# A chunked delta-rule attention with two MLPs on one Trainium2 core: the first group of chunks in another order, and nine idle-time matmuls during its inverse

## The chip, the cores and the metric

One core of a Trainium2 chip runs the whole program. The metric is device time in microseconds (us) of one execution, as a median of several; the profile is of one execution of its own.

## The reference, cut to what matters

```python
# attention: batch 4, heads 8, sequence 768, head size 48
for t in range(S):
    kt, vt, bt = (k_n[:, :, t], v[:, :, t], beta[:, :, t, None])
    y[:, :, t] = np.einsum('bhd,bhde->bhe', q[:, :, t], state)
    v_old = np.einsum('bhde,bhd->bhe', state, kt)
    state = state + bt[:, :, :, None] * np.einsum('bhd,bhe->bhde', kt, vt - v_old)
...
# first MLP: 8 experts over all 3072 tokens, weighted by a Sinkhorn-normalised gate P
for e in range(E):
    h = np.maximum(x @ w1[e], 0.0)
    ye = h @ w2[e]
    out += P[:, e:e + 1] * ye
...
# second MLP
h = x @ w_in
g = h * (1.0 / (1.0 + np.exp(-1.702 * h)))
return (g @ w_out).astype(np.float32)
```

k_n is k divided by its norm. The attention is a recurrence over the tokens; both MLPs take all 3072 tokens.

## The kernel before

The attention goes in 24 chunks `u` of 64 tokens, and the chunks in six groups `g` of four. All heads of two batches are taken together, on the upper and the lower 64 partitions. Two pieces of program make it up.

- `prep(g)` makes, for the four chunks of a group, the inverse of a triangular matrix. `gram` multiplies keys with keys and with queries on TensorE (tile `pg`); the scores times the mask `bm` go to `am` (`take`, L188), and the products with the queries to the planes of `x` (L199), which GpSimd masks later (`mask_m`, L207). The lower blocks of `am` are copied beside the diagonal (L266), a VectorE transpose makes `ln` (L269), and 30 steps of two VectorE instructions each, `lt` (L279) and `ln` (L283), invert the blocks. Two more transposes make `ta` (L314) and `tt` (L340); small matmuls `pz` (L323) and `px` (L332), each followed by ScalarE copies, finish the inverse in `tt`.
- `chain(u)` is the recurrence itself, in four stages: `ks` (keys times state, L373) and the right side `r` on VectorE (L375; in a first chunk minus `v`, on ScalarE, L379); `up` (inverse times `r`, L384) and its copies to `su`; `sp` (keys times `su`, L395) and the new state `S` (L399, L401); `y` (L408) and its copy `ys`. Each stage needs the one before it.

When chunk u is in work, the output of chunk u-1 is transposed (`xt`, L421) and split into two float32r parts `xb` (L495 on ScalarE, L496 on VectorE). From it come the gate's logits (`pl`) and the first expert (`expert0`, tiles `ph`, `po`), cut into items of three matmuls. Before expert 0 its weights are split: ScalarE casts them, and VectorE subtracts (L545, tiles `w1s`, `w2s`) in four sets of four instructions; `split0` is a call for the next set.

The order of the instructions on each engine is the order in which Python issues them. `slot(t)` runs once per stage of a chunk (t = 4u + stage), takes a number of pieces from `prep` and puts expert items between them. For t up to 15 that number is `FIRST[t]`, afterwards `PIECES[t % 16]`. `self.at` ties some calls to a step of the inverse, by group and step: (0, 20) issues the score products of chunks 4 to 7 ahead, into PSUM tiles that expert 0 uses later (`early`), and `kept[v]` is the masking that takes them.

Group 0 runs ahead of the loop, up to the first `px`; the rest of its pieces, in the list below, and group 1 come between the stages of the first four chunks:

```python
((pz, 0, 8), (tr, None), (tr, 0, 0, 8), (tr, 64, 0, 8), (px, 0, 8), (tr, 0, 8, 24),
 (tr, 64, 8, 24), (pz, 8, 8), (px, 8, 8), (pz, 16, 16), (px, 16, 16))
```

Here `pz` and `px` name a first block and a number of blocks; eight blocks are one chunk. The attention is followed by seven experts and the second MLP, which fill the rest of the time with large matmuls.

Of the kernel before, what the change touches and what calls it, by code (L numbers as in the profile page):

```python
# [9 lines left out]
F32 = mybir.dt.float32  # L10
# [11 lines left out]
H = 8  # L22
D = 48
# [5 lines left out]
PIECES = (4, 2, 2, 1, 2, 4, 4, 4, 4, 4, 4, 4, 3, 3, 2, 2)  # L29
ITEMS = (6, 5, 5, 5, 5, 5, 5, 5, 5, 5, 5, 6, 5, 5, 5, 5)  # L30

FIRST = (0, 4, 3, 2, 2, 2, 2, 3, 3, 4, 5, 5, 5, 4, 4, 4)


LAG = 10
# [5 lines left out]
class Attention:  # L41
# [130 lines left out]
    def gram(self, u, planes, h0, n, pool=None):  # L172
# [21 lines left out]
        if planes[-1] == 1:  # L194
            for b in range(2):
# [4 lines left out]
                else:  # L200
                    nc.vector.tensor_tensor(out=m, in0=ps[p, :, len(planes) - 1], in1=bm[p, hs], op=ALU.mult)

    def mask_m(self, u):
        for b in range(2):
            p = slice(64 * (1 - b), 64 * (1 - b) + 64)
            m = self.X[u // 2 % 4][p, 1 + b, u % 2]
            self.nc.gpsimd.tensor_tensor(out=m, in0=m, in1=self.bm[u][p], op=ALU.mult)  # L207

    def prep(self, g):

        nc, am, tt = self.nc, self.am, self.tt
        w, u = 2 * g, 4 * g
        if g == 0:
            self.square(0, nc.vector)
            self.square(1, nc.vector)
            self.norm(0)
            self.norm(1)
            self.weigh(0, 1)
            self.mask(0, eng=nc.vector)
            for v in range(1, 4):  # L220
                self.mask(v)
            for v in range(4):
                self.gram(v, (0,), 0, H, (self.psc, "c") if v < 2 else None)
            self.scale_v(0)
            self.scale_k(0)
            self.square(2)
            self.square(3)
            self.at = {(0, 13): lambda: [self.gram(v, (1,), 0, H) for v in range(4, 8)],
                       (0, 20): lambda: self.kept.update({v: self.gram(v, (0,), 0, H, self.early[v - 4])
                                                          for v in range(4, 8)}),  # L230
                       (0, 23): lambda: self.split0(), (1, 4): lambda: self.split0(), (1, 10): lambda: self.split0()}
            yield 1.0
        elif g == 1:
            self.weigh(2, 3)
            nc.gpsimd.tensor_copy(out=self.gate, in_=self.w[3][:, 1, 7:8])
            self.scale_k(1)
            self.mask_m(2)
            self.mask_m(3)
            yield 1.0
            for v in range(4, 8):  # L240
                self.mask(v, eng=nc.vector)
                self.kept[v]()
                if v % 2:
                    self.split0()
                yield 1.0
        else:
            for i in range(8):
                if i == 5:
                    self.mask(u + 3)
                self.gram(u + i // 2, (0, 1), i % 2 * 4, 4)  # L250
                if i == 1:
                    self.square(w + 1)
                elif i == 2:
                    self.norm(w + 1)
                elif i == 3:
                    self.weigh(w + 1)
                    self.mask(u + 2)
                elif i == 7:
                    self.scale_k(w)
                    self.scale_k(w + 1)  # L260
                yield 1.0
# [1 line left out]
        ln = self.one.tile([128, 32, 32], F32, tag="ln", name="ln")  # L263

        for q in (32, 96):
            (nc.vector.tensor_copy if g == 0 and q == 32 else nc.scalar.copy)(  # L266
                out=am[q:q + 32, :, 0:32], in_=am[q:q + 32, :, 32:64])
            yield 1.0
        nc.vector.transpose(out=ln, in_=am[:, :, 0:32].rearrange("p m t -> p t m"))  # L269
        if g == 0:  # L270
# [4 lines left out]
        for jj in range(1, 31):  # L275
# [4 lines left out]
                out=t3, in0=ln[:, jj + 1:32, jj:jj + 1].to_broadcast([128, nr, jj]),  # L280
# [47 lines left out]
        def px(m0, n):  # L328
# [6 lines left out]
            for q in (0, 64):  # L335
                nc.scalar.copy(out=tt[q:q + 32, m0:m0 + n, 32:64], in_=ps[q:q + 32])

        def tr(q, m0=0, n=32):
            if q is None:
                nc.vector.transpose(out=tt[:, :, 32:64].rearrange("p m t -> p t m"), in_=ln)  # L340
            else:
                nc.scalar.copy(out=tt[q:q + 32, m0:m0 + n, 0:32], in_=tt[q:q + 32, m0:m0 + n, 32:64])

        for f, *i in (((pz, 0, 16), (tr, None), (pz, 16, 16), (tr, 0), (tr, 64), (px, 0, 16), (px, 16, 16)) if g else
                      ((pz, 0, 8), (tr, None), (tr, 0, 0, 8), (tr, 64, 0, 8), (px, 0, 8), (tr, 0, 8, 24),
                       (tr, 64, 8, 24), (pz, 8, 8), (px, 8, 8), (pz, 16, 16), (px, 16, 16))):
            while f == tr and self.upped < u - 1:
                yield 1.0
            f(*i)
            if f == px and i[0] == 0:  # L350
                self.ready = g
                if g == 0:
                    self.norm(2)
                    self.norm(3)
            yield 1.0

    def chain(self, u):

        nc = self.nc
# [3 lines left out]
        x, tt, bk = self.X[w % 4], self.tt, self.bk[w % 4]  # L363
        tk = [slice(64, 128), slice(0, 64)]
        S = self.S
        r = self.wk.tile([128, H, D], F32, tag="r", name="r", bufs=1)

        su = self.wk.tile([128, 2, H, D], F32, tag="su", name="su", bufs=1)
        if not first:
            ks = self.psc.tile([128, H, D], F32, tag="c", name="ks")  # L370
            for h in range(H):
                for b in range(2):
                    nc.tensor.matmul(ks[tk[b], h], x[64 * b:64 * b + D, 0, j, h], S[64 * b:64 * b + D, h],  # L373
                                     start=True, stop=True)
            nc.vector.tensor_tensor(out=r, in0=ks, in1=self.V[w][:, j], op=ALU.subtract)  # L375
            nc.scalar.copy(out=su[0:64, 0], in_=S[0:64])
            nc.scalar.copy(out=su[64:64 + D, 1], in_=S[64:64 + D])
        else:
            nc.scalar.mul(r, self.V[w][:, j], -1.0)  # L379
        yield  # L380
        up = self.psc.tile([128, H, D], F32, tag="c", name="up")
# [7 lines left out]
        if not last:  # L389
            sp = self.psc.tile([128, H, D], F32, tag="c", name="sp")  # L390
            for h in range(H):
                for b in range(2):
# [3 lines left out]
                                     start=True, stop=True)  # L396
# [64 lines left out]
def kernel(  # L461
# [268 lines left out]
    while A.ready < 0:  # L730
        next(prep)
# [11 lines left out]
    def slot(t):  # L743

        n, k = rate * ITEMS[t % 16] if t >= LAG else 0, (PIECES if t > 15 else FIRST)[t % 16]
        if t == LAG:
            expert(BURST)
        i = 0
        while i < k:
            expert(n / (k + 1) * step[0])  # L750
            step[0] = next(prep, 1.0)
            i += step[0]
        expert(n / (k + 1))
# [440 lines left out]
```

## Time and profile before

| | |
|---|---|
| median of 3 runs | 2224.41 us (2222.56 to 2230.47) |
| profiled execution, its own time | 2232.75 us |
| its span in the trace | 2230.4 us |
| busy: TensorE, VectorE | 97%, 68% |
| busy: GpSimd, ScalarE | 49%, 48% |
| mean granted TensorE clock | 0.975 of full speed |

In the rows, PE is TensorE, DVE VectorE, ACT ScalarE, POOL GpSimd. Times count from the start of the span. Each matmul that is not a transpose and has plain float32 operands makes two records in the trace: the stage `up` is 16 matmuls in the program and 32 records. PEclk is the granted clock as a share of 2.4 GHz, so that 0.50 is 1.2 GHz.

### The profile page before, as it was taken

The numbers are of one execution on the slowest core, as the hardware profiler recorded it, in microseconds if no ns is written. First come the engines' busy times: TensorE is split into PE (matmuls) and PEld (weight loads), VectorE is DVE, ScalarE is ACT, GpSimd is POOL, SyncE is SP. The second block draws the span as 40 slices with busy tenths as digits, with TensorE's granted clock in tenths as the row PEclk, the third lists the DMA queues.
The fourth block names the chain that finished last, engine by engine and source line by source line (L and its number), as shares of the span: only waits on it lengthen the run. The fifth ranks groups of instructions, "written<-read, shape, count | busy, mean of one in ns | idle before, by whom it ended". The sixth has DMA issues, their size and how long they took to land.

```text
span 2230.4 us, 40903 instructions
## 1 busy us (share of the span) xinstructions
PE 2156.8 (97%) x15663; PEld 1953.7 (88%) x15663; DVE 1526.7 (68%) x2792; ACT 1068.0 (48%) x2126; POOL 1096.8 (49%) x1275
## 2 busy tenths in 40 slices
PE   5799999998999999999999999999999999999999
PEld 4778888896989999999999999999999989889998
DVE  7847775627777777767776777777775556776676
ACT  4334434434444544444445444455544446565554
POOL 4141123224776776666552656556665434662333
PEclk8689999998999999999999999999999999999999
DMA  6223333348335343333448655565554465567231
GB/s 159 51 62 81 105 100 102 90 127 294 136 115 184 124 168 136 115 144 110 159 164 275 185 178 182 170 200 178 188 199 143 136 239 164 172 192 246 92 121 50
DMA packets 229154, 336.74 MB, mean 151 GB/s; under 512 B 15648, under 2 KB 192416, under 8 KB 224800
## 3 DMA queue, kind: packets, MB, share of 16 engines
q1 hardware_dynamic: 228096, 332.86, 46.1%
q8 instruction: 123, 2.02, 0.4%
q10 hardware_dynamic: 864, 1.28, 0.2%
q14 instruction: 71, 0.58, 0.1%
HBM read 204.58 MB, written 129.50 MB: 150 GB/s over the span
## 4 chain that ended last, share of the span: by engine, by line
PE 85%; DVE 9%; DMA 2%; POOL 1%; ACT 1%; issue 1%; SPq 0%; POOLq 0%; ACTq 0%; DVEq 0%
PE po L501 14%; PE po L499 14%; PE po L500 14%; PE c L500 11%; PE c L501 11%; PE c L499 11%; DVE lt L279 3%; DVE ln L283 3%; PE ph L499 1%; PE pg L182 1%; PE ph L500 1%; PE ph L501 1%; PE y L408 1%; PE sp L395 1%; PE px L332 1%
## 5 line engine op out<-in xcount | busy, mean ns | idle before, releaser
L501 PE MATMUL po<-w2c,h 128*128 128x384 f32 x1728 | 586.6, 339 | 1.4 <-DVE h L1007 1.3
L500 PE MATMUL po<-w2c,h 128*128 128x384 f32 x1728 | 587.3, 340 | 0.0
L499 PE MATMUL po<-w2c,h 128*128 128x384 f32 x1728 | 578.5, 335 | 1.1 <-ACT h L1005 1.1
L1062 POOL TENSOR_TENSOR acc<-acc,ye 128x384 f32<-128x384 f32 x252 | 261.6, 1038 | 381.7 <-ACT ye L1061 329.6
L501 PE MATMUL c<-xt,w1c 128*128 128x512 f32 x1080 | 429.1, 397 | 2.0 <-POOL w1c L496 2.0
L499 PE MATMUL c<-xt,w1c 128*128 128x512 f32 x1080 | 424.5, 393 | 4.4 <-DVE f L1039 2.3
L500 PE MATMUL c<-xt,w1c 128*128 128x512 f32 x1080 | 428.0, 396 | 0.0
L1039 DVE TENSOR_TENSOR o<-o,c 128x512 f32<-128x512 f32 x288 | 197.5, 686 | 246.7 <-PE c L501 231.5
L1064 DVE SCALAR_TENSOR_TENSOR acc<-po,P,acc 128x384 f32<-128x384 f32 x420 | 258.2, 615 | 150.6 <-PE po L501 150.3
L499 PEld LDWEIGHTS po<-w2c,h 128*128 128x128 f32 x1728 | 324.9, 188 | 41.0 <-ACT h L1005 1.7
L500 PEld LDWEIGHTS po<-w2c,h 128*128 128x128 f32 x1728 | 323.8, 187 | 40.1
L501 PEld LDWEIGHTS po<-w2c,h 128*128 128x128 f32 x1728 | 325.0, 188 | 4.3 <-DVE h L1007 4.3
L1061 ACT ACTIVATE ye<-po,P 128x384 f32<-128x384 f32 x252 | 146.6, 582 | 372.1 <-PE po L501 359.3
L501 PEld LDWEIGHTS c<-xt,w1c 128*128 128x128 f32 x1080 | 202.3, 187 | 47.0 <-POOL w1c L496 2.8
L996 ACT ACTIVATE h<-f 128x512 fp32r<-128x512 f32 x224 | 133.9, 598 | 192.8 <-DVE f L1039 191.0
L499 PEld LDWEIGHTS c<-xt,w1c 128*128 128x128 f32 x1080 | 203.0, 188 | 18.8 <-DVE f L1039 3.1
L1039 DVE TENSOR_TENSOR f<-o,c 128x512 f32<-128x512 f32 x288 | 199.2, 692 | 20.7 <-PE c L501 3.6
L500 PEld LDWEIGHTS c<-xt,w1c 128*128 128x128 f32 x1080 | 203.0, 188 | 9.8
L1032 ACT COPY o<-c 128x512 f32<-128x512 f32 x288 | 163.6, 590 | 59.7 <-PE c L501 58.2
L496 POOL TENSOR_TENSOR w2c<-w2r,w2c 128x384 fp32r<-128x384 f32 x140 | 149.4, 1067 | 47.7 <-ACT w2c L495 47.4
L1074 POOL TENSOR_TENSOR acc<-acc,ye 128x384 f32<-128x384 f32 x84 | 92.7, 1104 | 156.6 <-ACT ye L1073 154.0
L998 DVE SCALAR_TENSOR_TENSOR h<-f,h 128x512 fp32r<-128x512 f32 x224 | 153.1, 683 | 21.2 <-ACT h L996 21.1
(177 smaller groups left out, 3410.2 us busy)
## 6 DMA issues: line engine op xcount, KB each, us to landing
w1c<-wd SPq DMA_DIRECT2D x210, 384.0 KB, 4.4
wd<-w1c SPq DMA_DIRECT2D x28, 1920.0 KB, 7.0
xs<-bo SPq DMA_DIRECT2D x184, 128.0 KB, 2.2
xt<-xs SPq DMA_DIRECT2D x46, 512.0 KB, 6.6
w2r<-in_w_dram SPq DMA_DIRECT2D x55, 384.0 KB, 6.0
wd<-wo SPq DMA_DIRECT2D x56, 256.0 KB, 2.9
w1r<-in_w_dram SPq DMA_DIRECT2D x28, 384.0 KB, 7.6
x<-in_kq_dram SPq DMA_DIRECT2D x24, 384.0 KB, 6.5
```

Of the source, the lines that this page charges most:

```text
L496: eng.tensor_tensor(out=dst_lo, in0=src, in1=dst_hi.bitcast(F32), op=ALU.subtract)
L499: nc.tensor.matmul(ps, lhs[0], rhs[0], start=start, stop=False, **kw)
L500: nc.tensor.matmul(ps, lhs[0], rhs[1], start=False, stop=False, **kw)
L501: nc.tensor.matmul(ps, lhs[1], rhs[0], start=False, stop=stop, **kw)
L996: nc.scalar.activation(out=h[:, 0], in_=src, func=ACTF.Relu)
L998: nc.vector.scalar_tensor_tensor(out=h[:, 1], in0=src, scalar=0.0, in1=h[:, 0].bitcast(F32), op0=ALU.max, op1=ALU.subtract)
L1032: nc.scalar.copy(out=o, in_=ps)
L1039: nc.vector.tensor_tensor(out=d, in0=o, in1=ps, op=ALU.add if how == "add" else ALU.subtract)
L1061: nc.scalar.mul(ye, ps, P[:, u, e:e + 1])
L1062: nc.gpsimd.tensor_tensor(out=a, in0=a, in1=ye, op=ALU.add)
L1064: nc.vector.scalar_tensor_tensor(out=a, in0=ps, scalar=P[:, u, e:e + 1], in1=a, op0=ALU.mult, op1=ALU.add)
L1074: nc.gpsimd.tensor_tensor(out=a, in0=a, in1=ye, op=ALU.add)
```

## The change

`r` of the first chunk is made in group 0's preparation. `pz` of all blocks comes ahead of the stage `sp`, and the copies `tr` and the `px` of blocks 8 to 31 come later. The masks and scores of chunks 4 to 7 (`second`, `take`) are issued with group 0's pieces instead of ahead of group 1. Both copies of `am` in group 1 are on VectorE. The four sets of weight subtractions stand at other places, three of them inside the second inverse. `FIRST` has other numbers. And `warm` adds nine matmuls, identity times keys, into a PSUM tile `pw` that nobody reads, issued at step 21 of the first inverse.

```diff
--- before.py
+++ after.py
@@ -29,7 +29,7 @@
 PIECES = (4, 2, 2, 1, 2, 4, 4, 4, 4, 4, 4, 4, 3, 3, 2, 2)
 ITEMS = (6, 5, 5, 5, 5, 5, 5, 5, 5, 5, 5, 6, 5, 5, 5, 5)
 
-FIRST = (0, 4, 3, 2, 2, 2, 2, 3, 3, 4, 5, 5, 5, 4, 4, 4)
+FIRST = (0, 2, 3, 2, 3, 3, 3, 3, 3, 4, 4, 4, 4, 4, 4, 4)
 
 
 LAG = 10
@@ -200,6 +200,12 @@
                 else:
                     nc.vector.tensor_tensor(out=m, in0=ps[p, :, len(planes) - 1], in1=bm[p, hs], op=ALU.mult)
 
+    def warm(self):
+
+        ps = self.psc.tile([128, 512], F32, tag="c", name="pw")
+        for _ in range(9):
+            self.nc.tensor.matmul(ps, self.ident, self.bk[0][:, 0:512], start=True, stop=True)
+
     def mask_m(self, u):
         for b in range(2):
             p = slice(64 * (1 - b), 64 * (1 - b) + 64)
@@ -222,28 +228,20 @@
             for v in range(4):
                 self.gram(v, (0,), 0, H, (self.psc, "c") if v < 2 else None)
             self.scale_v(0)
+            self.r = self.wk.tile([128, H, D], F32, tag="r", name="r", bufs=1)
+            nc.scalar.mul(self.r, self.V[0][:, 0], -1.0)
             self.scale_k(0)
             self.square(2)
             self.square(3)
             self.at = {(0, 13): lambda: [self.gram(v, (1,), 0, H) for v in range(4, 8)],
                        (0, 20): lambda: self.kept.update({v: self.gram(v, (0,), 0, H, self.early[v - 4])
                                                           for v in range(4, 8)}),
-                       (0, 23): lambda: self.split0(), (1, 4): lambda: self.split0(), (1, 10): lambda: self.split0()}
+                       (0, 21): self.warm,
+                       (0, 23): lambda: self.split0()}
+            for jj in (6, 11, 16):
+                self.at[1, jj] = lambda: self.split0()
             yield 1.0
-        elif g == 1:
-            self.weigh(2, 3)
-            nc.gpsimd.tensor_copy(out=self.gate, in_=self.w[3][:, 1, 7:8])
-            self.scale_k(1)
-            self.mask_m(2)
-            self.mask_m(3)
-            yield 1.0
-            for v in range(4, 8):
-                self.mask(v, eng=nc.vector)
-                self.kept[v]()
-                if v % 2:
-                    self.split0()
-                yield 1.0
-        else:
+        elif g > 1:
             for i in range(8):
                 if i == 5:
                     self.mask(u + 3)
@@ -263,8 +261,10 @@
         ln = self.one.tile([128, 32, 32], F32, tag="ln", name="ln")
 
         for q in (32, 96):
-            (nc.vector.tensor_copy if g == 0 and q == 32 else nc.scalar.copy)(
+            (nc.vector.tensor_copy if g == 1 or (g, q) == (0, 32) else nc.scalar.copy)(
                 out=am[q:q + 32, :, 0:32], in_=am[q:q + 32, :, 32:64])
+            if (g, q) == (1, 96):
+                self.split0()
             yield 1.0
         nc.vector.transpose(out=ln, in_=am[:, :, 0:32].rearrange("p m t -> p t m"))
         if g == 0:
@@ -335,6 +335,24 @@
             for q in (0, 64):
                 nc.scalar.copy(out=tt[q:q + 32, m0:m0 + n, 32:64], in_=ps[q:q + 32])
 
+        def second():
+            self.norm(2)
+            self.norm(3)
+            self.weigh(2, 3)
+            nc.gpsimd.tensor_copy(out=self.gate, in_=self.w[3][:, 1, 7:8])
+            self.mask_m(2)
+            self.mask_m(3)
+            self.scale_k(1)
+            self.mask(4, eng=nc.vector)
+            self.kept[4]()
+            self.mask(5, eng=nc.vector)
+
+        def take(*vs):
+            for v in vs:
+                if v > 5:
+                    self.mask(v, eng=nc.vector)
+                self.kept[v]()
+
         def tr(q, m0=0, n=32):
             if q is None:
                 nc.vector.transpose(out=tt[:, :, 32:64].rearrange("p m t -> p t m"), in_=ln)
@@ -342,16 +360,14 @@
                 nc.scalar.copy(out=tt[q:q + 32, m0:m0 + n, 0:32], in_=tt[q:q + 32, m0:m0 + n, 32:64])
 
         for f, *i in (((pz, 0, 16), (tr, None), (pz, 16, 16), (tr, 0), (tr, 64), (px, 0, 16), (px, 16, 16)) if g else
-                      ((pz, 0, 8), (tr, None), (tr, 0, 0, 8), (tr, 64, 0, 8), (px, 0, 8), (tr, 0, 8, 24),
-                       (tr, 64, 8, 24), (pz, 8, 8), (px, 8, 8), (pz, 16, 16), (px, 16, 16))):
+                      ((pz, 0, 8), (tr, None), (tr, 0, 0, 8), (tr, 64, 0, 8), (px, 0, 8), (second,),
+                       (pz, 8, 8), (pz, 16, 16), (take, 5, 6), (tr, 0, 8, 24), (tr, 64, 8, 24), (px, 8, 8),
+                       (take, 7), (px, 16, 16))):
             while f == tr and self.upped < u - 1:
                 yield 1.0
             f(*i)
-            if f == px and i[0] == 0:
+            if f in (px, second) and (g > 0 or f == second) and i[0:1] in ([0], []):
                 self.ready = g
-                if g == 0:
-                    self.norm(2)
-                    self.norm(3)
             yield 1.0
 
     def chain(self, u):
@@ -363,7 +379,7 @@
         x, tt, bk = self.X[w % 4], self.tt, self.bk[w % 4]
         tk = [slice(64, 128), slice(0, 64)]
         S = self.S
-        r = self.wk.tile([128, H, D], F32, tag="r", name="r", bufs=1)
+        r = self.wk.tile([128, H, D], F32, tag="r", name="r", bufs=1) if u else self.r
 
         su = self.wk.tile([128, 2, H, D], F32, tag="su", name="su", bufs=1)
         if not first:
@@ -375,7 +391,7 @@
             nc.vector.tensor_tensor(out=r, in0=ks, in1=self.V[w][:, j], op=ALU.subtract)
             nc.scalar.copy(out=su[0:64, 0], in_=S[0:64])
             nc.scalar.copy(out=su[64:64 + D, 1], in_=S[64:64 + D])
-        else:
+        elif u:
             nc.scalar.mul(r, self.V[w][:, j], -1.0)
         yield
         up = self.psc.tile([128, H, D], F32, tag="c", name="up")
```

What this does to the order, at three places. TensorE first, from the last product of queries and keys to the first `sp` (`sp` goes on in 14 more rows). Before:

```order
L182 MATMUL pg<-x_128 64x64 x32
L323 MATMUL pz<-ta,am 32x32 x16
L332 MATMUL px<-tt,ta 32x32 x16
L384 MATMUL up<-r,tt 64x48 x16
L323 MATMUL pz<-ta,am 32x32 x16
L332 MATMUL px<-tt,ta 32x32 x16
L395 MATMUL sp<-su,bk_147 64x48
L395 MATMUL sp<-su,bk_147 48x48
```

With the change:

```order
L182 MATMUL pg<-x_128 64x64 x32
L207 MATMUL pw<-bk_147,ident 128x512 x9
L323 MATMUL pz<-ta,am 32x32 x16
L332 MATMUL px<-tt,ta 32x32 x16
L400 MATMUL up<-r,tt 64x48 x16
L323 MATMUL pz<-ta,am 32x32 x48
L411 MATMUL sp<-su,bk_147 64x48
L411 MATMUL sp<-su,bk_147 48x48
```

`pw` is new, the second `px` is gone from between `pz` and `sp`, and all of `pz` stands there. The rows behind that `sp`, to the first `xt`, before:

```order
L323 MATMUL pz<-ta,am 32x32 x32
L332 MATMUL px<-tt,ta 32x32 x32
L408 MATMUL y<-su,x_125 64x48 x16
L373 MATMUL ks<-S,x_125 64x48 x16
L384 MATMUL up<-r,tt 64x48 x16
L421 MATMUL xt<-ident,ys 128x128 x3
```

and with the change:

```order
L424 MATMUL y<-su,x_125 64x48 x16
L332 MATMUL px<-tt,ta 32x32 x16
L389 MATMUL ks<-S,x_125 64x48 x16
L332 MATMUL px<-tt,ta 32x32 x32
L400 MATMUL up<-r,tt 64x48 x16
L437 MATMUL xt<-ident,ys 128x128 x3
```

`y` and `ks` now stand ahead of most of `px`.

VectorE, from the masks of the last chunks of group 1 to the transpose that begins its inverse (`bm` is a mask, `am` takes the scores, `w1s` and `w2s` are weight subtractions). Before:

```order
L375 TENSOR_TENSOR r<-ks,v 128x384
L168 TENSOR_TENSOR bm<-nmask,wt 128x512
L188 TENSOR_TENSOR am<-pg,bm 128x512
L168 TENSOR_TENSOR bm<-nmask,wt 128x512
L188 TENSOR_TENSOR am<-pg,bm 128x512
L545 TENSOR_TENSOR w1s_191<-wr,w1s_191 128x384
L545 TENSOR_TENSOR w1s_192<-wr,w1s_192 128x384
L545 TENSOR_TENSOR w2s_199<-wr,w2s_199 128x384
L545 TENSOR_TENSOR w2s_200<-wr,w2s_200 128x384
L496 TENSOR_TENSOR xb<-xt,xb 128x3x128
L401 TENSOR_TENSOR S<-S,sp 112x384
L269 STREAM_TRANSPOSE ln<-am 128x1024
```

With the change:

```order
L188 TENSOR_TENSOR am<-pg,bm 128x512
L168 TENSOR_TENSOR bm<-nmask,wt 128x512
L188 TENSOR_TENSOR am<-pg,bm 128x512
L391 TENSOR_TENSOR r<-ks,v 128x384
L264 COPY am<-am 32x32x32 x2
L561 TENSOR_TENSOR wgs<-wgr,wgs 128x3x8
L561 TENSOR_TENSOR w1s_189<-wr,w1s_189 128x384
L561 TENSOR_TENSOR w1s_190<-wr,w1s_190 128x384
L561 TENSOR_TENSOR w2s_197<-wr,w2s_197 128x384
L561 TENSOR_TENSOR w2s_198<-wr,w2s_198 128x384
L512 TENSOR_TENSOR xb<-xt,xb 128x3x128
L269 STREAM_TRANSPOSE ln<-am 128x1024
```

The masks stand ahead of `r`, the copies of `am` behind it, one set of weights instead of two is left ahead of the transpose, and `S` has gone behind it.

ScalarE, from the copies of the first `px` to the copy of the first state. Before:

```order
L336 COPY tt<-px 32x8x32 x2
L129 ACTIVATE ns<-ss 128x16 x2
L379 ACTIVATE r<-v 128x384
L385 COPY su<-up 64x384
L386 COPY su<-up 64x384
L342 COPY tt<-tt 32x24x32 x2
L326 COPY ta<-pz 32x256 x2
L336 COPY tt<-px 32x8x32 x2
L399 ACTIVATE S<-sp 112x384
```

With the change:

```order
L336 COPY tt<-px 32x8x32 x2
L129 ACTIVATE ns<-ss 128x16 x2
L401 COPY su<-up 64x384
L402 COPY su<-up 64x384
L326 COPY ta<-pz 32x256 x2
L326 COPY ta<-pz 32x512 x2
L415 ACTIVATE S<-sp 112x384
```

`r` is gone from ahead of the copies `su`, and the long copies of `tt` from ahead of `ta` and `S`.

## Rows read from the trace of the kernel before

**Rows 1.** The page: busy time, share of the span and instructions of TensorE.
```profile
PE 2156.8 (97%) x15663; PEld 1953.7 (88%) x15663; DVE 1526.7 (68%) x2792; ACT 1068.0 (48%) x2126; POOL 1096.8 (49%) x1275
```

**Rows 2.** Chain that ended last, 60 to 80 us: start, us, what.
```profile
74.90 1.04 ACT am L266
...
77.03 1.94 DVE ln L269
```

**Rows 3.** Timeline, 47 to 53 us: start, us, instruction, count, idle before and releaser.
```profile
47.21 2.00 DVE L340 STREAM_TRANSPOSE tt<-ln 128x1024 f32<-128x1024 f32 x1
47.56 1.07 PE L323 MATMUL pz<-ta,am 32*32 32x32 f32 x32 [8.64 <-DVE ta L314]
...
49.36 1.17 PE L332 MATMUL px<-tt,ta 32*32 32x32 f32 x32 [0.73 <-DVE tt L340]
...
50.62 0.75 ACT L336 COPY tt<-px 32x256 f32<-32x256 f32 x2 [0.35 <-PE px L332]
...
51.62 0.51 ACT L379 ACTIVATE r<-v 128x384 f32<-128x384 f32 x1
...
52.18 1.94 PE L384 MATMUL up<-r,tt 64*64 64x48 f32 x32 [1.65 <-ACT r L379]
```

**Rows 4.** Timeline, 54 to 73 us.
```profile
54.94 1.30 DVE L168 TENSOR_TENSOR bm<-nmask,wt 128x512 f32<-128x512 f32 x1
...
57.15 1.45 PE L332 MATMUL px<-tt,ta 32*32 32x32 f32 x32 [2.03 <-ACT ta L326]
...
59.35 4.59 DVE L545 TENSOR_TENSOR w2s<-wr,w2s 128x384 fp32r<-128x384 f32 x2
...
60.39 1.92 PE L323 MATMUL pz<-ta,am 32*32 32x32 f32 x64
...
68.81 0.56 DVE L375 TENSOR_TENSOR r<-ks,v 128x384 f32<-128x384 f32 x1 [4.88 <-PE ks L373]
69.29 0.68 DVE L168 TENSOR_TENSOR bm<-nmask,wt 128x512 f32<-128x512 f32 x1
...
71.94 1.02 DVE L545 TENSOR_TENSOR w1s<-wr,w1s 128x384 fp32r<-128x384 f32 x2
```

**Rows 5.** Timeline, price of one `am` copy and of three `xt`.
```profile
20.10 1.04 ACT L266 COPY am<-am 32x1024 f32<-32x1024 f32 x1 [10.71 <-DVE am L188]
20.10 1.19 DVE L266 COPY am<-am 32x1024 f32<-32x1024 f32 x1
...
71.39 0.90 PE L421 MATMUL xt<-ident,ys 128*128 128x128 f32 x3
```

**Rows 6.** Instructions of tile `xt`: ns min/median/max, first and last start us.
```profile
L421 PE MATMUL xt<-ident,ys x72: 270/272/473, 71.4 to 492.2; 128*128 128x128 f32 x72
```

**Rows 7.** Busy time by stretch (1, 2 and 10 us), PEclk the granted clock.
```profile
42.00:43.00 1.00, 0.00 (x0) 0.00 (x0) 0.90 (x4) 0.31 (x1) 0.00 (x0) 0.60 0.00 0
...
74.00:76.00 2.00, 2.00 (x36) 1.88 (x33) 0.87 (x2) 1.57 (x3) 0.00 (x0) 0.50 0.03 8
...
140.00:150.00 10.00, 10.00 (x88) 8.00 (x87) 3.50 (x8) 0.49 (x2) 5.58 (x5) 0.56 0.46 139
```

**Rows 8.** Timeline, 79 to 116 us: the second inverse and the first expert items.
```profile
79.04 0.17 DVE L279 TENSOR_TENSOR lt<-ln 128x30 f32<-128x30 f32 x1
...
88.12 0.56 DVE L496 TENSOR_TENSOR xb<-xt,xb 128x384 fp32r<-128x384 f32 x1 [1.54 <-ACT xb L495]
...
89.43 0.38 PE L499 MATMUL pl<-xb,wgs 128*8 128x256 f32 x1
...
105.87 1.14 PE L384 MATMUL up<-r,tt 64*64 64x48 f32 x32 [2.11 <-DVE r L375]
...
112.88 2.06 DVE L314 STREAM_TRANSPOSE ta<-ln 128x1024 f32<-128x1024 f32 x1
...
115.00 1.20 PE L323 MATMUL pz<-ta,am 32*32 32x32 f32 x64 [1.83 <-DVE ta L314]
```

**Rows 9.** Sum of 40 stretches of 10 us, 110 to 510 us.
```profile
sum 400.00, PE 383.16 PEld 340.97 DVE 235.70 ACT 163.91 POOL 103.24; mean PE 9.58 PEld 8.52 DVE 5.89 ACT 4.10 POOL 2.58
```

## Prediction

> **What bounds the kernel now.** The page's busy times come first: TensorE is busy for 97% of the span [rows 1], so a change can gain only where it waits or runs slowly. Summed over 110 to 510 us it is busy for 383.16 of 400 us [rows 9], and the MLPs behind that are denser still. The loose end is the start. There the chain of waits goes another way: to 77 us it ends on ScalarE's two copies of `am`, then VectorE's transpose [rows 2], and the second inverse begins at 79.04 [rows 8]. The timeline tells why. TensorE idles 8.64 us until the first `ta` [rows 3], so from 38.92 to 47.56; its clock falls within 42 to 43 us (0.60 is a mean over that microsecond), and the stretch 74 to 76 still shows 0.50, with TensorE busy throughout [rows 7]. The recurrence of the first chunk then runs stage by stage at 1.2 GHz, and VectorE waits 4.88 us for `ks` [rows 4]. Expert work, the filler of TensorE, begins at 89.43 with `pl` [rows 8].
>
> So I price the change by two instants: when the second inverse begins, and when TensorE gets its first expert item. What they move, everything behind moves by, as long as TensorE stays full.
>
> **The `warm` matmuls.** A transpose is one record: three of 128 columns take 0.90 us, the longest single one of tile `xt` is 0.473 [rows 5, 6]. I estimate from both a spacing of (0.90 - 0.47) / 2 = 0.21 us at 1.2 GHz, so 0.11 at 2.4. Four times as many columns give 0.43 us at 2.4 GHz, 0.85 at 1.2. A plain float32 matmul makes two records, so nine make 18: 7.7 us at 2.4 GHz, 15.4 at 1.2; with one record each 3.8 would be the low end. I take 7.7, because the clock has not yet fallen when TensorE goes idle at 38.92 (a mean of 0.60 puts the fall near 42.2). Then `pw` ends at 46.6, and `pz` waits for `ta` until 47.5 anyway: they cost nothing, and the cover is that idle time. At 15.4 they end at 54.3, and `pz` comes 6.8 us late.
>
> What do they give? The first `pz` gets faster, but `px` must wait for `tt`, 47.21 + 2.00 [rows 3], so that is worth nothing. `px` itself, 1.17 us, would save 0.5 if the clock lasts to 50 us; I count 0.3 of it. For the rest of the group I take 1.2 GHz: in 74 to 76 us TensorE is busy all the time with such small matmuls, and the clock stays at 0.50 [rows 7].
>
> The Trainium skill has a rule that says otherwise (TensorE: Matmul & The Clock Gate, "Why this matters for your kernels"): whoever leaves no idle gaps between bursts avoids the throughput drop. By it the whole group would run at 2.4 GHz, and the gain would be that of the second rival below; the stretch at 74 us speaks against it.
>
> **`r` early.** It takes 0.51 us of ScalarE between the first `px` copies (end 51.37) and `up` (52.18) [rows 3]. Its new place is in an idle time of 10.71 us of ScalarE [rows 5], so it is free there. `up` starts at 51.4, with the 0.3 above at 51.1: 1.1 us earlier.
>
> **`pz` up, `px` down.** Now TensorE waits 2.03 us for the copies `ta` behind the long copies of `tt`, and spends 1.45 on `px` ahead of `sp` [rows 4]. In the new order it goes on without a wait. Prices at 1.2 GHz: a stage of 32 records 1.94 us [rows 3], 64 of `pz` 1.92 [rows 4], so 96 about 2.9. `up` 51.1 to 53.0, `pz` to 55.9 (the copies `su` lie under it), `sp` to 57.9, `y` to 59.8, eight blocks of `px` to 61.0, `ks` to 62.9. The state copy and the rest of ScalarE's queue lie under `y` and `px`. So `r` of the second chunk comes at 63.0 instead of 68.81: 5.8 us earlier. The rest of `px`, 1.9 us, stands behind `ks`, where VectorE makes `r`: no loss.
>
> **Masks and scores ahead of `r`.** Two pairs of `bm` and `am` move from behind `r` (69.29 to 71.94, so 2.65 us [rows 4]) into the wait ahead of it. All four pairs cost 5.3 us undisturbed, from about 53.5 (the second `bm` is at 54.94, one pair behind the first). But GpSimd now masks `x` at that time, and rows show what VectorE pays beside it: `bm` 1.30 instead of 0.68, and two weight subtractions 4.59 instead of 1.02 [rows 4]. With three `bm` at 1.30 the pairs end at 53.5 + 5.3 + 3 x 0.62 = 60.7, before `ks`; at the worst price, 2.30 each, at 63.7, 0.7 late. I take the first: no cost, and the cover is `ks`.
>
> **`am` copies on VectorE.** On ScalarE they stood behind `xt`'s copies and ended at 77.0 [rows 2]. Now two of 1.19 us [rows 5] follow `r` (63.6): 66.0. One set of weights, 2.2 us from two times 1.02 [rows 4] and a small one, to 68.2. `xb` has to wait for `up` and `xt` (`px` to 64.8, `up` to 66.7, 0.47 and 0.5 us of copies on ScalarE twice over): 69.0. The transpose, 1.94, ends at 71.0. The second inverse begins at 71.0 instead of 79.04: **8.0 us earlier**.
>
> **What is given back.** The inverse took 112.88 - 79.04 = 33.84 us [rows 8]. One more set of weights now stands inside, +2.0; the wait of 1.54 for `xb` [rows 8] goes, since `xb` now stands after eleven steps instead of seven. TensorE sees less of it: `r` of the third chunk stands further down, after eight steps and a set, near 79.7; `up`, `xt`, `sp` follow, and `pl` comes near 85.1, 4.3 us earlier. VectorE then waits about 1.0 us for the first experts' `ph`. The sum at `ta`: 8.0 - 2.0 + 1.5 - 1.0 = **6.5 us** earlier, so near 106.4. TensorE arrives with 4.3, and its waits of 2.11 and 1.83 us for VectorE on the way to `pz` [rows 8] shrink by about as much as is lacking, so that `pz` also comes 6.5 us earlier. From there TensorE is full, and the shift lasts to the end.
>
> **Later groups.** They start one piece earlier, and their `pz` stands an expert item or so sooner; each engine's work is the same. Between gains and losses I take 0. Queues: SP carries the same transfers but for places; GpSimd has `mask_m` and `scale_k` swapped, and `bk` is wanted only by `sp` at 83 us.
>
> **The sum.** The profiled execution took 2232.75 us, so by its own time 2226.3; it lies 8.3 above the runs' median, and I set the gain against that: 2224.4 - 6.5 = 2217.9.
>
> **Rivals.**
> 1. *The gain is absorbed.* If the first experts hold up VectorE (`h` waits for `ph`) or `r` comes later than I place it, `pl` at 4.3 us is the whole shift and less survives. For it: TensorE, not VectorE, carries 110 to 510 us. Against it: TensorE's waits of 2.11 and 1.83 are on VectorE. Gain 0 to 3: 2223.
> 2. *The clock holds through the first group.* Then `ks` ends near 57 us, the masks (60.7) set `r`, and the inverse begins near 68.7, 2.3 us earlier than above; the first `ph` at full speed add some 1.5. Gain 10.3: 2214. Against it stands 74 to 76 us [rows 7].
> 3. *A drop of the clock goes.* In 140 to 150 us the clock was 0.56 [rows 7]: at half speed nearly throughout, 0.44 x 10 = 4.4 us lost. With fewer waits ahead, this one and a shorter one may not happen: gain 11 to 13, 2212. It may as well come at another place.
> 4. *Slower: `pw` outlasts its cover.* If it starts at 1.2 GHz, or its weight loads don't overlap, it takes 15.4 us or more, `pz` starts at 54.3, and all behind is 6.8 us late: 6.5 - 6.8, so 0.3 lost; at 20 us of `pw`, 5 lost: 2229. It decides from about 15 us, 1.7 for each of the nine. Against it: the granted clock at 39 us had not fallen.
>
> That the nine do nothing for the clock is inside the forecast: it costs 0.3.
>
> **Chances.** Forecast (gain 3 to 10) 0.58, absorbed 0.16, clock holds 0.10, fewer drops 0.11, slower 0.05. The range from 2207 to 2227 leaves out the far end of the slower case and of the faster ones. 0.5% is 11.1 us, about what a measurement can tell: faster needs under 2213.3, which is most of fewer drops, some of the held clock and a tail of the forecast, 0.19; slower by as much is a corner of rival 4, 0.02; within, 0.79.
>
> **What would show it.** `pw` with 18 records from about 39 to 47 us at PEclk 1.00; `up` at 51.1 with no `r` ahead; no wait of TensorE between `up` and `ks`; masks done before `r` near 63; the second inverse from 71, `pl` near 85, the second `ta` near 106. Wrong if `pz` starts after 48, if the inverse starts after 74, or if the 6.5 us at `ta` are gone by 500 us.

## The result and the profile after

The changed kernel took **2250.61 us** (median of 4 runs, 2248.31 to 2257.29) against 2223.48 for the kernel before on the same chip: a ratio of **1.0122, 95% interval 1.0102 to 1.0142**. It is slower by 1.2%, and outside the range given. The profiled execution took 2251.81 us, its span 2249.5; its mean granted clock, 0.975, is that of the profiled execution of before. Over all timed executions the changed kernel has 0.970 to 0.976 and the kernel before 0.975 to 0.983.

The first group went nearly as the prediction has it. Timeline of the changed kernel, 38 to 111 us (start, us, instruction, count, idle before and releaser); it answers to [rows 3, 4, 8]:

```profile
38.17 7.99 PE L207 MATMUL pw<-bk,ident 128*128 128x512 f32 x18
...
47.15 0.69 PE L323 MATMUL pz<-ta,am 32*32 32x32 f32 x32 [0.99 <-DVE ta L314]
...
50.52 1.95 PE L400 MATMUL up<-r,tt 64*64 64x48 f32 x32 [0.89 <-ACT tt L336]
...
52.40 2.77 PE L323 MATMUL pz<-ta,am 32*32 32x32 f32 x96
...
59.29 1.95 PE L389 MATMUL ks<-S,x 48*64 48x48 f32 x32
59.62 3.38 DVE L168 TENSOR_TENSOR bm<-nmask,wt 128x512 f32<-128x512 f32 x1 [1.71 <-POOL x L213]
...
63.72 0.55 DVE L391 TENSOR_TENSOR r<-ks,v 128x384 f32<-128x384 f32 x1
...
64.30 1.39 DVE L264 COPY am<-am 32x1024 f32<-32x1024 f32 x2
...
68.83 1.96 DVE L269 STREAM_TRANSPOSE ln<-am 128x1024 f32<-128x1024 f32 x1
...
84.39 0.38 PE L515 MATMUL pl<-xb,wgs 128*8 128x256 f32 x1
...
107.23 2.07 DVE L314 STREAM_TRANSPOSE ta<-ln 128x1024 f32<-128x1024 f32 x1
109.36 1.20 PE L323 MATMUL pz<-ta,am 32*32 32x32 f32 x64 [1.56 <-DVE ta L314]
```

`pw` ends at 46.16 and hides in TensorE's wait. The second inverse begins at 71, 8 us earlier than before, and the second `ta` at 107.23 stands 5.65 us ahead of the 112.88 in [rows 8]. Up to here the change is a gain.

The loss lies behind it. The starts of the five later `ta` (VectorE, L314), read from the timeline, before against after:

| group | 1 | 2 | 3 | 4 | 5 |
|---|---|---|---|---|---|
| before | 112.88 | 192.21 | 267.54 | 341.65 | 416.67 |
| after | 107.23 | 188.72 | 267.66 | 350.05 | 435.98 |
| lead | 5.65 | 3.49 | -0.12 | -8.40 | -19.31 |

From `ta` to `ta`, groups 3 to 5 take 78.9, 82.4 and 85.9 us instead of 75.3, 74.1 and 75.0. Behind the attention nothing more changes: the first matmul of the dense part (`c`) starts at 553.55 instead of 534.14, so 19.4 us late. (The profiled execution of before lies 9.3 us above the median of 2223.48, that of the changed kernel 1.2 above its own, hence 19 here and 27 between the medians.)

What happens shows at chunk 15, in which the inverse of group 4 ends. The kernel before, timeline of TensorE and VectorE:

```profile
339.69 0.49 DVE L375 TENSOR_TENSOR r<-ks,v 128x384 f32<-128x384 f32 x1
...
341.33 1.13 PE L384 MATMUL up<-r,tt 64*64 64x48 f32 x32
341.65 2.13 DVE L314 STREAM_TRANSPOSE ta<-ln 128x1024 f32<-128x1024 f32 x1
342.86 0.49 PE L421 MATMUL xt<-ident,ys 128*128 128x128 f32 x3
...
343.90 0.56 DVE L496 TENSOR_TENSOR xb<-xt,xb 128x384 fp32r<-128x384 f32 x1
343.93 1.20 PE L323 MATMUL pz<-ta,am 32*32 32x32 f32 x64 [0.58 <-DVE ta L314]
344.37 2.03 DVE L340 STREAM_TRANSPOSE tt<-ln 128x1024 f32<-128x1024 f32 x1
```

The changed kernel, the same place:

```profile
348.75 0.55 DVE L391 TENSOR_TENSOR r<-ks,v 128x384 f32<-128x384 f32 x1
...
350.05 2.05 DVE L314 STREAM_TRANSPOSE ta<-ln 128x1024 f32<-128x1024 f32 x1
352.15 1.20 PE L323 MATMUL pz<-ta,am 32*32 32x32 f32 x64 [2.13 <-DVE ta L314]
...
354.05 1.95 PE L400 MATMUL up<-r,tt 64*64 64x48 f32 x32
...
356.73 0.84 PE L437 MATMUL xt<-ident,ys 128*128 128x128 f32 x3
...
358.12 0.56 DVE L512 TENSOR_TENSOR xb<-xt,xb 128x384 fp32r<-128x384 f32 x1 [6.03 <-ACT xb L511]
...
358.60 1.95 DVE L358 STREAM_TRANSPOSE tt<-ln 128x1024 f32<-128x1024 f32 x1
```

Before, TensorE does `up` and `xt` while VectorE makes `ta`: `pz` waits 0.58 us. After, the first `pz` is issued ahead of `up`. The new `FIRST` takes 50 pieces in the first four chunks instead of 52, but what is left of groups 0 and 1 now counts 49 instead of 52. So groups 2 to 5 stand one piece ahead, and in the first stage of chunks 7, 11, 15 and 19 that piece is `pz`. TensorE takes its instructions in order: it waits 2.13 us for `ta`, with `up` behind, whose `r` has been there since 349.3. `xt` is late in turn, VectorE waits 6.03 us for `xb`, and `tt`, which stands behind it, starts 8.55 us after `ta` instead of 2.72. And `up`, 1.13 us before, takes 1.95: TensorE has fallen to half its clock. Stretches of 20 us of the changed kernel (the stretch, TensorE's busy time and instructions, then PEclk, the granted clock):

```profile
270.00:290.00 20.00, 20.00 (x383) 0.74 0.30 68
350.00:370.00 20.00, 17.87 (x356) 0.74 0.28 77
```

The same stretches in the kernel before, where the clock stays up:

```profile
270.00:290.00 20.00, 20.00 (x439) 1.00 0.34 71
350.00:370.00 20.00, 19.92 (x359) 1.00 0.32 72
```

The sum of all twenty stretches from 110 to 510 us of the changed kernel has TensorE busy for 373.99 of 400 us, where [rows 9] have 383.16:

```profile
sum 400.00, PE 373.99; mean PE 18.70
```

### The profile page after: what moved, and what is told of

Same layout as the page of the kernel before. It is cut to its first block, busy times and chain, and to the rows that moved or that the text cites. A ratio compares the mean times of both kernels' runs of the same rounds, so it can differ in the third digit from the quotient of the medians.

```text
span 2249.5 us, 40929 instructions
## 1 busy us (share of the span) xinstructions
PE 2170.4 (96%) x15681; PEld 1961.5 (87%) x15681; DVE 1525.0 (68%) x2794; ACT 1067.1 (47%) x2124; POOL 1096.6 (49%) x1275
## 4 chain that ended last, share of the span: by engine, by line
PE 82%; DVE 10%; DMA 3%; POOL 2%; issue 2%; ACT 1%; SPq 0%; POOLq 0%; ACTq 0%; DVEq 0%
PE po L517 14%; PE po L516 14%; PE po L515 14%; PE c L516 10%; PE c L517 10%; PE c L515 10%; DVE lt L279 2%; DVE ln L283 2%; PE ph L515 1%; PE up L400 1%; PE pg L182 1%; PE ph L516 1%; PE ph L517 1%; PE pz L323 1%; DMA w1r<-in_w_dram 1%
## 5 line engine op out<-in xcount | busy, mean ns | idle before, releaser
L515 PEld LDWEIGHTS c<-xt,w1c 128*128 128x128 f32 x1080 | 202.9, 188 | 19.4 <-DVE f L1055 3.9
L1014 DVE SCALAR_TENSOR_TENSOR h<-f,h 128x512 fp32r<-128x512 f32 x224 | 153.1, 683 | 20.9 <-ACT h L1012 20.8
```

Of the source, the lines that this page charges most:

```text
L515: nc.tensor.matmul(ps, lhs[0], rhs[0], start=start, stop=False, **kw)
L1014: nc.vector.scalar_tensor_tensor(out=h[:, 1], in0=src, scalar=0.0, in1=h[:, 0].bitcast(F32), op0=ALU.max, op1=ALU.subtract)
```

## The experiments

All were timed against the kernel before on the same chip (2223.0 to 2226.3 us there). The first theory was the one just told: **`pz` ahead of `up`** holds the recurrence up. Its rivals were the nine matmuls, and loss by contention or the clock with no one place.

**e1_realign.** The changed kernel, groups 2 to 5 put back by one piece.

```diff
-FIRST = (0, 2, 3, 2, 3, 3, 3, 3, 3, 4, 4, 4, 4, 4, 4, 4)
+FIRST = (0, 2, 3, 2, 3, 3, 3, 3, 3, 4, 4, 4, 4, 4, 4, 3)
```

> The change with the last number of FIRST 3 instead of 4, so that groups 2 to 5 stand as in the kernel before and only the first two groups differ. Theory A (the loss is that the pieces of groups 2 to 5 stand one piece ahead of the recurrence): the lead of some 6 us at the second ta (107.3 against 112.9) is kept to the end, 2215 to 2220. Rival B (the loss comes from the new first group itself, by the clock or by what it leaves on the engines): 2240 or more, as the change has it. Rival C (the lead is absorbed later whatever the order is): 2222 to 2226.

Measured: 2222.15 us, ratio 0.9983 (0.9971 to 0.9995). One piece in one slot takes the whole loss away. The time is in rival C's range and not in theory A's: of the 5.2 us of lead at group 1, 4 us (1 to 6) by the ratio reach the end; more on that below.

**e2_pz_ahead.** The kernel before, with the piece ahead in groups 2 to 5 and nothing else of the change.

```diff
-PIECES = (4, 2, 2, 1, 2, 4, 4, 4, 4, 4, 4, 4, 3, 3, 2, 2)
+PIECES = (4, 2, 2, 1, 2, 4, 4, 4, 4, 4, 4, 4, 4, 2, 2, 2)
```

> The kernel before with PIECES[12] 4 and PIECES[13] 2 instead of 3 and 3: in groups 2 to 5 only the first pz moves, from behind up to ahead of it; the inverse, the scores and the first group stay. Theory A1 (TensorE waits for ta at pz with up behind it, and VectorE then waits for xb and tt): most of the loss, 2240 to 2250. Rival A2 (the whole group standing one piece ahead is what costs, the inverse and the scores too): under 2230.

Measured: 2253.64 us, ratio 1.0122 (1.0104 to 1.0139): the loss of the whole change, from this piece alone, and 4 us more than the theory's range. Its timeline at chunk 11:

```profile
271.66 2.05 DVE L314 STREAM_TRANSPOSE ta<-ln 128x1024 f32<-128x1024 f32 x1
...
273.77 1.55 PE L323 MATMUL pz<-ta,am 32*32 32x32 f32 x64 [2.84 <-DVE ta L314]
...
276.50 1.95 PE L384 MATMUL up<-r,tt 64*64 64x48 f32 x32
...
281.37 2.00 DVE L340 STREAM_TRANSPOSE tt<-ln 128x1024 f32<-128x1024 f32 x1
```

**e3_no_warm.** The changed kernel without the nine matmuls (the line `(0, 21): self.warm` taken out).

> The change without the nine matmuls pw. Theory A: they do next to nothing, since up is cold either way: 2250 to 2254. Rival B (they shift the clock's falls, and the later drops come from that): back towards 2225 to 2235.

Measured: 2256.64 us, ratio 1.0140 (1.0119 to 1.0162). The loss stays; the nine are not its cause.

**e4_before_ahead.** The kernel before, the last number of `FIRST` 5 instead of 4, which puts groups 2 to 5 one piece ahead as the change does.

> The kernel before with the last number of FIRST 5 instead of 4: groups 2 to 5 stand one piece ahead, as in the change, the first two groups are as before. Theory A: the loss without the lead, 25 to 33 us over the kernel before, 2248 to 2257. Rival B: no more than 5 us over it, under 2229.

Measured: 2254.41 us, ratio 1.0127 (1.0110 to 1.0143), as expected.

**e5_realign_no_warm.** e1 without the nine matmuls.

> The realigned change without the nine matmuls pw. If pw only makes the first px and the copies behind it earlier, 0 to 2 us over the realigned change: 2222 to 2225. If pw also moves later falls of the clock, up to 5 us either way.

Measured: 2218.25 us, ratio 0.9975 (0.9963 to 0.9988), some us below what was expected and not to be told from e1. The nine give nothing that can be measured.

**e7_pz_held.** The changed kernel; `pz`, too, waits for `up` to be issued.

```diff
-            while f == tr and self.upped < u - 1:
+            while f in (tr, pz) and self.upped < u - 1:
```

> The change as it is, FIRST included, with one condition more: a pz of a later group waits, as tr does, until the up of the chunk before its group is issued. The waiting takes one piece, so that the rest of each group falls back in step. Theory A1 (pz ahead of up is the loss): 2216 to 2226, with the realigned change. Rival (the scores and the inverse of the second group, a piece ahead, cost as well): 2230 to 2240.

Measured: 2226.12 us, ratio 1.0012 (0.9996 to 1.0029; its runs scatter from 2219 to 2238.6). The loss is gone but for what can't be told from none.

**e8_fill.** e2, and three matmuls of identity and keys into `pz`'s own tile ahead of the first `pz` of groups 2 to 5, to see how much of the loss is the clock. Nobody reads what they write.

```diff
+            for _ in range(3 if g > 1 and m0 == 0 else 0):
+                nc.tensor.matmul(ps.rearrange("p m s -> p (m s)"), self.ident, self.bk[w % 4][:, 0:512],
+                                 start=True, stop=True)
```

> The kernel before with pz ahead of up (as in e2_pz_ahead), and three matmuls of identity and keys in front of the first pz of groups 2 to 5, 3 x 0.85 us, which fill TensorE's wait for ta. Theory: about half of the loss is TensorE's clock falling after that wait, the other half the wait itself; with the wait filled the clock stays, and about half of the 29 us comes back: 2236 to 2242. Rival (the loss is the recurrence standing late, the clock follows from other waits): no gain, 2252 to 2260.

Measured: 2239.75 us, ratio 1.0065 (1.0046 to 1.0084). Work was added, and about half of the loss went. Its timeline at chunk 11:

```profile
267.78 2.73 PE L322 MATMUL pz<-bk,ident 128*128 128x512 f32 x6
...
270.86 1.20 PE L326 MATMUL pz<-ta,am 32*32 32x32 f32 x64 [0.34 <-DVE ta L314]
...
272.71 1.14 PE L387 MATMUL up<-r,tt 64*64 64x48 f32 x32
...
275.92 1.99 DVE L343 STREAM_TRANSPOSE tt<-ln 128x1024 f32<-128x1024 f32 x1
```

`pz` comes no sooner after `ta` than in e2, but `up` takes 1.14 us instead of 1.95, and `tt` starts 7.2 us after `ta` instead of 9.7.

**e9_am_on_act.** e1 with the two copies of `am` of group 1 on ScalarE again.

```diff
-            (nc.vector.tensor_copy if g == 1 or (g, q) == (0, 32) else nc.scalar.copy)(
+            (nc.vector.tensor_copy if (g, q) == (0, 32) else nc.scalar.copy)(
```

> The realigned change with the two copies of am in group 1 back on ScalarE. If the move to VectorE carries the lead at the second inverse, 2 to 4 us of it go: 2224 to 2227, and the transpose ln starts near 72 to 73 instead of 69.3. If the masks ahead of r carry it, nothing changes: 2220 to 2224.

Measured: 2220.86 us, ratio 0.9983 (0.9971 to 0.9994), with the transpose `ln` at 68.89 us as in the changed kernel: the engine of the copies makes no difference.

**e10_plain_order.** The edits of e5 and e9 together, so that only the new order of group 0, masks and weight sets is left.

> The changed kernel with the last number of FIRST 3 instead of 4, without the nine matmuls, and with the two copies of am in group 1 on ScalarE again: of the change only the new order of group 0's pieces and of masks, scores and weight sets is left. Theory (the loss is the early pz, the small gain comes from the order of the first group alone, and the nine matmuls and the copies add nothing): 2216 to 2222 us, ratio to before 0.996 to 0.9995, ta of group 1 between 107 and 109 us. Rival (the copies or the nine matmuls carry a part of the gain together): 2222 to 2226, ta of group 1 after 110 us.

Measured: 2218.29 us, ratio 0.9968 (0.9955 to 0.9981), `ta` of group 1 at 107.33. The order of the first group is enough for the gain. This version is 0.3% faster than the kernel before and has the lowest ratio here, but its interval overlaps those of e1, e5 and e9.

**e11_pz_later.** The kernel before, shifted the other way: `PIECES[12]` is 2 and `PIECES[13]` is 4, so that `ta` moves behind `r` and `xb` on VectorE and `pz` stays behind `up`.

> The kernel before with PIECES[12] = 2 and PIECES[13] = 4: in chunks 7, 11, 15 and 19 the transposes ta move one stage down, from ahead of the chunk's right side r to behind it on VectorE; pz keeps its stage, behind up. Theory (what costs is a wait on TensorE with up behind it; here up comes no later): pz waits a little longer for ta, some 1 to 2 us in each of four groups with nothing urgent behind it, 2222 to 2232 us, ratio 0.999 to 1.004. Rival (the order of group and chunk is so finely balanced that a shift of a piece in either direction costs the same): 2245 to 2255.

Measured: 2253.87 us, ratio 1.0125 (1.0104 to 1.0147). **Here the first theory fell**: `up` follows its `r` after 1.1 us (0.6 before), ahead of `pz`, and the loss is just the same. Timeline at chunk 11:

```profile
271.73 1.14 PE L384 MATMUL up<-r,tt 64*64 64x48 f32 x32
...
274.47 0.56 DVE L496 TENSOR_TENSOR xb<-xt,xb 128x384 fp32r<-128x384 f32 x1 [2.13 <-ACT xb L495]
274.95 2.03 DVE L314 STREAM_TRANSPOSE ta<-ln 128x1024 f32<-128x1024 f32 x1
...
277.13 1.91 PE L323 MATMUL pz<-ta,am 32*32 32x32 f32 x64 [3.20 <-DVE ta L314]
```

Now VectorE waits for TensorE's `xt`, by way of ScalarE's half of `xb`, before it can start `ta`, and TensorE then waits 3.20 us for `ta`, with `pz` at half clock behind (1.91 instead of 1.20). What e2 and e11 share is that `ta` no longer runs beside `up` and `xt`, so that TensorE stands still at the first `pz`.

**e6_one_behind.** The changed kernel, the last number of `FIRST` 2 instead of 4: all pieces of groups 2 to 5 one place behind those of the kernel before, by way of the other constant.

> The changed kernel with the last number of FIRST 2 instead of 4: groups 2 to 5 stand one piece behind those of the kernel before, so that ta and the first pz are issued together behind up, and the last px falls into the next chunk's first stage, ahead of its up. Theory (only pz ahead of up costs): 2220 to 2232 us, ratio 0.998 to 1.004. Rival (any shift of the order costs as much): 2245 to 2255. A third case: ready for the next group is set by the first px, which is still in time; if the second px makes up of the next group late, 2230 to 2240.

Measured: 2250.67 us, ratio 1.0111 (1.0093 to 1.0129): again the whole loss, against the theory. At chunk 11 `ta` stands behind `xb`, and `pz` waits 2.85 us. e1 and e7, for their part, also fit the second theory below: in both `ta` runs beside `up` again.

**e12_ta_twice.** So the second theory: **a standstill of TensorE of 2 to 3 us at the first `pz`, and the clock that falls with it, whatever the order that brings it about**. The test leaves the order of before untouched and only makes `ta` longer.

```diff
-        nc.vector.transpose(out=ta.rearrange("p m s -> p s m"), in_=ln.rearrange("p t s -> p s t"))
+        for _ in range(2 if g > 1 else 1):
+            nc.vector.transpose(out=ta.rearrange("p m s -> p s m"), in_=ln.rearrange("p t s -> p s t"))
```

> The kernel before, its order untouched, with the transposes ta of groups 2 to 5 made twice, so that the first pz of these groups waits about 2.0 us longer for VectorE, up being done by then. Theory (what costs is a wait of TensorE of some 2 to 3 us at the first pz, whatever the order that causes it, and the clock then falls for the small matmuls behind it): sum of the waits of pz on ta between 110 and 520 us from 4.8 to some 13 us, clock below 0.85 in the 20 us behind each, 2238 to 2256 us, ratio 1.006 to 1.014. Rival 1 (only the wait counts): four times 2.0 us, 2230 to 2233. Rival 2 (only an order that holds up the recurrence costs): 2222 to 2227.

Measured: 2245.94 us, ratio 1.0090 (1.0072 to 1.0108). At chunk 11:

```profile
273.39 1.13 PE L385 MATMUL up<-r,tt 64*64 64x48 f32 x32
...
274.11 4.25 DVE L315 STREAM_TRANSPOSE ta<-ln 128x1024 f32<-128x1024 f32 x2
...
278.50 1.72 PE L324 MATMUL pz<-ta,am 32*32 32x32 f32 x57 [2.40 <-DVE ta L315]
```

Four times 2.1 us of VectorE cost 20 us by the ratio (16 to 24), some 5 us each. In the 20 us behind the four waits the mean clock was 0.68, 0.75, 0.91 and 0.74, so below the expected 0.85 in three of them; the kernel before has 0.91, 1.00, 1.00 and 0.83 there. Both rivals of this run are out.

The table sets the runs side by side. The wait is TensorE's before `pz` for `ta` in groups 2 to 5. Idle is 400 us less TensorE's busy time in twenty stretches of 20 us from 110 to 510 us; clock is the sum over them of 20 x (1 - PEclk), an estimate of what the lower clock cost. Then comes the time from `ta` of group 1 to the first `c` in the same trace; the ratio is that of the timed runs.

| kernel | wait of `pz` | idle | clock | `ta` to `c` | ratio |
|---|---|---|---|---|---|
| before | 3.0 | 16.8 | 17.6 | 421.3 | 1 |
| change | 9.1 | 26.0 | 31.2 | 446.3 | 1.0122 |
| e2_pz_ahead | 11.2 | 24.8 | 29.4 | 441.7 | 1.0122 |
| e3_no_warm | 9.4 | 27.0 | 31.0 | 447.1 | 1.0140 |
| e4_before_ahead | 9.1 | 28.4 | 31.2 | 444.6 | 1.0127 |
| e6_one_behind | 11.9 | 28.2 | 32.6 | 447.3 | 1.0111 |
| e11_pz_later | 12.5 | 27.3 | 32.8 | 444.6 | 1.0125 |
| e12_ta_twice | 11.3 | 26.2 | 29.2 | 438.6 | 1.0090 |
| e8_fill | 1.7 | 15.2 | 20.8 | 433.3 | 1.0065 |
| e1_realign | 2.9 | 17.6 | 17.4 | 420.6 | 0.9983 |
| e5_realign_no_warm | 3.3 | 18.8 | 10.4 | 413.7 | 0.9975 |
| e7_pz_held | 2.8 | 21.0 | 10.4 | 417.8 | 1.0012 |
| e9_am_on_act | 3.3 | 20.7 | 8.6 | 414.5 | 0.9983 |
| e10_plain_order | 3.5 | 20.1 | 10.2 | 416.2 | 0.9968 |

The kernels with the loss have 8 to 12 us more idle time than before and 12 to 15 us more of the clock, together 20 to 26 us, and from `ta` to `c` they take 17 to 26 us longer; those without it have next to nothing more in the two columns together. e8 has only 2 us more in them, and some 10 us of added matmuls (four times 2.7) for the rest of its 12. In e12 the wait of `pz` grew by 8.3 us (and by 1.5 in group 1, which the edit leaves alone) and all idle time by 9.4, so on balance nothing else stood still: the rest is the clock, 11.6 by its column. In the changed kernel the wait grew by 6.1 and the other idle time by 5: mostly waits for VectorE, above all of `pg` for `x` (L201; 0.87, 1.44 and 2.34 us), some 30 us behind a `pz`. That the late `up` and `xt` bring these about is not shown.

## Why the prediction was wrong

- **Right: `pw`, and what it gives.** 18 records in 7.99 us (7.7 forecast), ended by 46.16 (46.6), hidden, and worth nothing that can be measured (e3, e5). `up` came at 50.52, 0.6 us ahead of the 51.1 forecast: 0.4 because `px` started earlier than before, 0.2 because the clock stayed up to 49.7 us and `px` took 0.69. Rival 2 fell: the clock fell at 49.7 us, within a stretch, 46.16 to 50.52 us, in which TensorE was busy for 1.39 us between waits of 0.99, 1.09 and 0.89. From `up` to `ks` it then had work without a gap of a microsecond, and still

```profile
40.00:50.00 10.00, 7.55 (x79) 3.69 (x77) 9.45 (x20) 3.07 (x9) 4.74 (x5) 0.99 0.00 0
50.00:60.00 10.00, 9.48 (x238) 9.17 (x240) 7.26 (x24) 6.33 (x15) 7.44 (x7) 0.50 0.14 43
```

  (The columns are the stretch, the busy time of TensorE, its weight loads, VectorE, ScalarE and GpSimd, PEclk and DMA: from 50 us on TensorE is busy 9.48 of 10 us at 0.50, that is at 1.2 GHz.) The rule of the Trainium skill (TensorE: Matmul & The Clock Gate, "Why this matters for your kernels"), that matmul bursts without long idle gaps between them are spared the throughput drop, is not borne out here: no gap between `pw` and the fall was longer than 1.09 us.
- **Right, in part by luck: the first group.** `ks` ended at 61.2 instead of 62.9, the masks at 63.8 instead of 60.7 (one `bm` took 3.38 us, more than the 2.30 set as the worst), the copies of `am` 1.39 together instead of 2.38. The errors cancel (`ks` came early, and the masks, put at no cost, set `r`): `r` 63.7 (63.0), the second inverse 71 (71.0), `pl` 84.4 (85.1), `ta` 107.2 (106.4). The lead at `ta` was 5.65 us against the 6.5 of the sum. To the end, e1, which is the change with its later groups put back, gains 0.17%, 4 us (1 to 6); e10 gains 0.32%, 7 us (4 to 10); the runs can't tell the two apart.
- **Not needed: the `am` copies on VectorE.** Their new engine is no part of the gain: on ScalarE (e9) they end at 67.0 us, and the transpose behind them starts right behind `xb`, at 68.89 us there and at 68.83 in the changed kernel. That they are the end of the chain [rows 2] held only in the old order.
- **Wrong: "Later groups. They start one piece earlier, and their `pz` stands an expert item or so sooner; each engine's work is the same. Between gains and losses I take 0."** The work is the same, but one piece is not an expert item: it is the place of `pz` on the far side of `up`. Put at 0, that term measured some 30 us (e2, 1.22%; e1 against the change, 1.4%), and by e12 the reason is that TensorE stands still for 2 to 3 us in each of four groups, which with the half clock behind it comes to 5 to 8 us a group. The nearest row was in sight: in group 1 `pz` waits 1.83 us for `ta` [rows 8]. Had I asked of each later group, as I did of the first, what TensorE has to do while VectorE transposes, I would have found `up` behind the wait.
- **Wrong: the bounds.** The slower rival was bound to `pw` and ended at 2229; none was about the groups that the shift touches four times over, and a loss of 0.5% or more had a chance of 0.02. Of the prediction's own signs of being wrong the last came true: the lead at `ta` was gone by 268 us.

What stays open: e1, e5, e9 and e10 have the change's 5 to 6 us of lead at group 1 in their traces, but their medians differ (0.17 to 0.32% below before) by no more than their intervals, and in e1 the lead was 5.8 us at group 4, 2.0 at the last `up` and 5.8 at the first `c`. The clock column of e5, e7, e9 and e10 is 7 to 9 us below that of before, that of e1 is not. Whether the new order spares the clock there, as the prediction's third rival has it, or the executions differ by themselves, one trace of each can't tell. Where e7's lead went is not settled: its profiled execution is 13 us shorter than that of before, its median is not.

## What to carry to other kernels

When a list of pieces is consumed by counts, one piece more or less at the start shifts everything behind it: find in the order of the instructions what the shift moves past what, in each later round, and price the waits there. Here the handover from VectorE to TensorE was cheap where the producer's long instruction (`ta`) lay beside other work of the consumer (`up`, `xt`), and a shift in either direction broke that (e2, e11). And a standstill of 2 us ahead of small matmuls cost more than twice itself (e12), since they went on at half clock.

## What the runs showed of the hardware

- The `bm` at 59.62 us, 0.69 us at its shortest, took 3.38, to 63.00. GpSimd's rows at that time, in the timeline of the changed kernel:

```profile
59.55 1.47 POOL L162 TENSOR_TENSOR bk<-bk,wt 128x768 f32<-128x768 f32 x1
60.98 1.47 POOL L113 TENSOR_TENSOR v<-v,nn 128x768 f32<-128x768 f32 x1
```

  The Trainium skill (SBUF — State Buffer, "SBUF: two separate sides") calls the ports that VectorE and GpSimd share an exclusive lock, held for a whole instruction. The trace agrees, and one VectorE instruction was held here for two of GpSimd's: they end at 62.45, and 0.55 us later so does `bm`.
- The copies of `am` took 0.69 us each on VectorE where GpSimd was idle, and 1.19 in [rows 5], beside GpSimd's `sq` (L122).
- About half of the loss of a badly placed wait was the clock, and in e8 most of that half came back (the clock column has 20.8, against 29.4 in e2 and 17.6 before): with TensorE kept busy by matmuls that nobody reads, `up` ran in 1.14 us instead of 1.95.
